# A mixture-of-experts loop: the next rows of a full block turned by VectorE in 16 pieces instead of by TensorE, and a slot table of one packed word

## The chip, the cores and the metric

One Trainium2 chip, one of its cores. The metric is the device time of one execution in microseconds; lower is better. The core's engines run side by side, each through its own queue in order: TensorE (PE, with its weight loads listed apart as PEld), VectorE (DVE), ScalarE (ACT), GpSimd (POOL) and SyncE (SP, which here mostly issues transfers).

## The reference

Eight batches of twelve heads, 448 tokens each, head width 64: sigmoid attention, whose output becomes 3584 rows of 768. A skip score and a gate then pick, for each row that is computed at all, one of eight experts; the others stay as they are.

```python
scores = scale * q @ k.T - log(S);  attn = sigmoid(scores);  x = attn @ v   # -> rows [3584, 768]
do = x @ w_skip > 0
e  = argmax(x[do] @ w_gate);  g = softmax weight of e
out = x;  out[do] = x[do] + g * (relu(x[do] @ w1[e]) @ w2[e])               # w1 [8,768,1024], w2 [8,1024,768]
```

How many rows each expert gets is known only on the chip, so the expert part is a loop whose blocks are chosen at run time.

## The kernel before

**Stages.** The attention fills the first half of the span and something more. While it runs, rows are written to `out`, and records (token number and gate weight) are sorted by expert into a list in DRAM. VectorE then computes a table of blocks ("slots"), while TensorE works through two first blocks of the largest early expert. After them comes the loop (L1549), one block an iteration, up to 128 rows of one expert in a block.

**Four kinds of block.** `FULL` and `SPLIT` (`block(i, last)`, L1347, with `last` False and True) compute 128 rows with weights split into a high and a low part, three matmuls in place of one, for precision: `gemm1` (L508) in 18 matmuls for each half of the hidden width, `gemm2` (L538) in six for each of eight slices `j`. `SPLIT` is the last full block before the expert changes: it also makes the high and low weights of the next expert, on ScalarE and VectorE. `HALF` (up to 64 rows, L1464) and `FEW` (up to 32, L1404) use unsplit weights of an expert of their own, which SP fetches for a later block while they run (`load_w1`, `load_w2`). The planner mixes them so that weights can arrive: in this run the loop goes SPLIT, HALF, FULL, HALF, FULL, FEW, FULL, FEW, FULL, FEW, SPLIT, FEW, FULL, FEW.

**What a FULL block does, in TensorE's order:** `gemm1(0)`; the first nine matmuls of `gemm1(1)`; `turn_h(0)` (four transposes of the hidden half 0); the other nine; `turn_x` of `xn`, the rows of the next block (six transposes of 128x128 into PSUM tiles `pxt`, L492); `gemm2(0)`; `turn_h(1)`; `gemm2(1)` to `gemm2(7)`. The order is written by hand (`tc.manual_schedule()`), so each engine's queue is in the order of the text.

**Around it.** ScalarE's `relu` and VectorE's share of `split_h` (L536) make `hh`/`hl`, the left operands of `gemm2`; each slice of `gemm2` uses `hl` in its last two matmuls. `ready_x` (L1120) reads the turned rows and makes `xh`, `xl`, `xf`, the next block's operands. `fetch` (L1279, on POOL) waits until `xn` has been read, then gathers the rows of the block after the next into `xn` and its records into `rn`; `take_rec` copies the records. At the end VectorE weighs the sums into `ys` (L1345, in a FEW block `yt`, L1460), `put` scatters them by an indirect transfer that adds (L570), and `advance` shifts the records. VectorE reaches a block only after it has finished this tail of the block before. In a FEW block the write of `yt` waits for the scatter of the block before.

**The table.** `slots` holds three numbers a slot: whether the block fetches an expert, which, and the kind. `entry` (L1103) loads one of them to a register. Every engine loads the kind at the head of an iteration; in HALF and FEW blocks SP loads the two others as well.

## Time and profile before

| | us |
|---|---|
| median of 3 runs (lowest, highest) | 528.02 (527.29, 532.5) |
| profiled execution, whole | 530.13 |
| its span, first to last instruction | 525.3 |
| TensorE busy in the span | 504.4 |
| VectorE busy | 293.4 |
| ScalarE busy | 272.3 |
| POOL busy | 259.0 |

The profile shows one execution. Its own time is 4.8 us above its span and 2.1 us above the median; differences are worked out within the span and then put on the median. In a timeline row the first number is the start in us, the second the time from the start of the first to the end of the last instruction of the row. The chain is followed back from the last instruction, at each step to what released it.

### The profile page before, as it was taken

The numbers are of one execution on the slowest core, as the hardware profiler recorded it, in microseconds if no ns is written. First come the engines' busy times: TensorE is split into PE (matmuls) and PEld (weight loads), VectorE is DVE, ScalarE is ACT, GpSimd is POOL, SyncE is SP. The second block draws the span as 40 slices with busy tenths as digits, with TensorE's granted clock in tenths as the row PEclk, the third lists the DMA queues.
The fourth block names the chain that finished last, engine by engine and source line by source line (L and its number), as shares of the span: only waits on it lengthen the run. The fifth ranks groups of instructions, "written<-read, shape, count | busy, mean of one in ns | idle before, by whom it ended". The sixth has DMA issues, their size and how long they took to land.

```text
span 525.3 us, 15167 instructions
## 1 busy us (share of the span) xinstructions
PE 504.4 (96%) x4982; PEld 332.6 (63%) x4983; DVE 293.4 (56%) x744; ACT 272.3 (52%) x480; POOL 259.0 (49%) x405
## 2 busy tenths in 40 slices
PE   8999999989999999999999999999999999999992
PEld 5555545545455555555555989948678787878771
DVE  4665647646668678488575862862122222249431
ACT  5776766757567666676675212942112323258311
POOL 5524463442555876667566332553224444446543
PEclk9999999999999999999999999999999999999997
DMA  7798576577688887878764133979393959595953
GB/s 235 180 266 216 157 180 156 147 161 194 170 223 219 211 204 221 196 193 251 193 125 100 17 93 122 375 226 334 97 372 117 347 199 350 203 351 203 327 190 47
DMA packets 139713, 107.23 MB, mean 204 GB/s; under 512 B 96263, under 2 KB 112265, under 8 KB 139664
## 3 DMA queue, kind: packets, MB, share of 16 engines
q1 hardware_dynamic: 133264, 97.66, 62.9%
q0 software_dynamic: 4736, 8.66, 7.3%
q8 instruction: 32, 0.52, 0.4%
q10 hardware_dynamic: 1664, 0.26, 0.3%
q14 instruction: 17, 0.14, 0.1%
HBM read 98.49 MB, written 17.60 MB: 221 GB/s over the span
## 4 chain that ended last, share of the span: by engine, by line
PE 92%; ACT 3%; DMA 2%; issue 1%; DVE 1%; POOLq 0%; POOL 0%; DVEq 0%; ACTq 0%
PE s L236 26%; PE pa L264 23%; PE py L543 11%; PE ph L516 10%; PE b_ph L516 3%; PE b_py L543 3%; PE py L1412 2%; DMA out_dram<-ys,rp 2%; PE ph L1412 2%; PE py L1470 2%; PE ph L1470 2%; PE pxt L492 2%; ACT at L256 2%; PE pl L296 2%; PE pht L530 1%
## 5 line engine op out<-in xcount | busy, mean ns | idle before, releaser
L256 ACT ACTIVATE at<-s,bias 128x896 f32<-128x896 f32 (+1 forms) x191 | 170.6, 914 | 85.0 <-PE s L236 79.1
L236 PE MATMUL s<-x 64*64 64x448 f32 (+1 forms) x1504 | 160.9, 497 | 5.8 <-ACT at L256 5.0
L264 PE MATMUL pa<-at,v 64*64 64x448 f32 (+1 forms) x1528 | 162.0, 489 | 0.0
L180 POOL COPY kq<-kq 32x896 f32<-32x896 f32 (+1 forms) x96 | 87.9, 915 | 80.3 <-DMA kq<-in_q_dram 41.8
L236 PEld LDWEIGHTS s<-x 64*64 64x64 f32 x1504 | 76.0, 191 | 62.2 <-ACT at L256 28.3
L264 PEld LDWEIGHTS pa<-at,v 64*64 64x64 f32 x1528 | 59.7, 133 | 57.8 <-issue 52.1
L216 DVE STREAM_TRANSPOSE x<-kq 128x448 f32<-128x448 f32 x94 | 82.1, 949 | 8.9 <-POOL kq L180 5.6
L274 DVE TENSOR_TENSOR xt<-xt,pa 128x448 f32<-128x448 f32 x48 | 29.8, 620 | 68.1 <-ACT xt L680 61.7
L486 POOL TENSOR_TENSOR wl<-wr,wh 128x384 fp32r<-128x384 f32 (+1 forms) x28 | 31.3, 1124 | 26.9 <-DVE wh L485 18.7
L413 POOL DMA_INDIRECT lst<-rec,idx x32 | 32.4, 1012 | 18.3 <-issue 13.5
L279 DVE STREAM_TRANSPOSE y<-xt 128x448 f32<-128x448 f32 x48 | 31.0, 646 | 1.6
L536 DVE TENSOR_TENSOR hl<-pht,hh 128x512 fp32r<-128x512 f32 x14 | 9.7, 690 | 37.6 <-ACT hh L535 32.7
L525 ACT ACTIVATE hs<-ph 128x512 f32<-128x512 f32 x14 | 8.4, 597 | 42.0 <-PE ph L516 34.1
L543 PE MATMUL py<-wh,hh 128*128 128x384 f32 x112 | 29.9, 348 | 0.0
L543 PE MATMUL py<-wh,hl 128*128 128x384 f32 x112 | 28.8, 338 | 0.2 <-DVE hl L536 0.2
L543 PE MATMUL py<-wl,hh 128*128 128x384 f32 x112 | 28.7, 337 | 0.0
L680 ACT ACTIVATE xt<-pa 128x448 f32<-128x448 f32 x48 | 25.7, 536 | 3.1 <-PE s L236 1.8
L516 PE MATMUL ph<-wl,xh 128*128 128x512 f32 x84 | 26.6, 403 | 0.0
L502 DVE TENSOR_TENSOR xl<-pxt,xh 128x384 fp32r<-128x384 f32 x30 | 15.3, 552 | 19.1 <-issue 9.6
L516 PE MATMUL ph<-wh,xh 128*128 128x512 f32 x84 | 25.7, 403 | 0.0
L1345 DVE TENSOR_SCALAR ys<-py,recs 128x384 f32<-128x384 f32 (+1 forms) x18 | 10.4, 612 | 26.0 <-PE py L543 20.7
L516 PE MATMUL ph<-wh,xl 128*128 128x512 f32 x84 | 24.4, 395 | 0.0
(291 smaller groups left out, 681.8 us busy)
## 6 DMA issues: line engine op xcount, KB each, us to landing
raw<-in_moe_w_dram SPq DMA_DIRECT2D x64, 768.0 KB
v<-in_v_dram SPq DMA_DIRECT2D x47, 256.0 KB
out_dram<-y SPq DMA_DIRECT2D x192, 56.0 KB
kq<-in_k_dram SPq DMA_DIRECT2D x23, 448.0 KB
kq<-in_q_dram SPq DMA_DIRECT2D x23, 448.0 KB
wr<-in_moe_w_dram SPq DMA_DIRECT2D x12, 256.0 KB
wr<-in_moe_w_dram SPq DMA_DIRECT2D x16, 192.0 KB
lst<-fill SPq DMA_DIRECT2D x4, 464.0 KB
```

The source lines that it names most:

```text
L180: nc.gpsimd.tensor_copy(a[to, :, :, :BT], a[at, :, :, BT:])
L216: nc.vector.transpose(xs[:, n].rearrange("p (r j) -> p j r", j=NJ), t.rearrange("p (j d) -> p j d", d=D)[:, :, :BT],)
L236: nc.tensor.matmul(sc[m * D : (m + 1) * D, j, : qs.stop - qs.start], xs[r, 0, first::NR7], xs[r, 1, qs], start=True, stop=True,)
L256: nc.scalar.activation(at[:, :, :n], sc[:, :, :n], AF.Sigmoid, bias=bias, scale=SCALE)
L264: nc.tensor.matmul(pa[j * D : (j + 1) * D, r, qs], vt[r][j][:, c if r == j else (c + 1) % NV, :], at[rs, j, : qs.stop - qs.start], start=( ...
L274: nc.vector.tensor_tensor(x, x, pa[:, 1, :S], op=ALU.add)
L279: nc.vector.transpose(y, xts[b][:, hp, :])
L413: put = nc.gpsimd.indirect_dma_start(out=lst[:, :], out_offset=bass.IndirectOffsetOnAxis(ap=idx[:, c : c + 1], axis=0), in_=rec[:, c, :], ...
L486: nc.gpsimd.tensor_tensor(lo, r, hi, op=ALU.subtract)
L516: nc.tensor.matmul(ph[h], a[:, j * P : (j + 1) * P], w[j][h], start=(n == 0), stop=(n == len(t) - 1),)
L543: last = nc.tensor.matmul(py[:, o, :H2], a[h][:, js], w[j][:, o * H2 : (o + 1) * H2], start=(j == 0 and n == 0), stop=(j == NK2 - 1 and n ...
L680: nc.scalar.activation(xts[b][:, hp, :], pa[:, 0, :S], AF.Copy)
```

## The change

In FULL blocks VectorE turns the next rows. `xn` (128 tokens by 768 columns) is taken in 16 pieces: 32 tokens by 192 columns, the columns being six runs of 32. One `transpose` turns its six 32x32 squares and writes them to one group of 32 partitions of a new tile `xw` in SBUF. Twelve pieces stand at the head of the block, ahead of everything VectorE does in it; four behind `take_rec`. `gemm2(0)` and `gemm2(1)` both stand ahead of `turn_h(1)`. `ready_x` reads `xw` there. The other three kinds turn as before. A slot is one word: 32 times the kind, plus 16 if an expert is fetched, plus the expert; SP takes the two fields out of the word that it loaded already.

```diff
+    W = 4 * NE
-    V.tensor_scalar(at5[:, 4], at5[:, 4], float(HALF - FEW), float(FEW), op0=ALU.mult, op1=ALU.add)
+    V.tensor_scalar(
+        at5[:, 4], at5[:, 4], float(W * (HALF - FEW)), float(W * FEW), op0=ALU.mult, op1=ALU.add
+    )
...
     V.tensor_reduce(at5[:, 2:4], w3d[:, 0:2], axis=AX.X, op=ALU.add)
+    V.scalar_tensor_tensor(
+        at5[:, 4], at5[:, 2], float(2 * NE), at5[:, 4], op0=ALU.mult, op1=ALU.add
+    )
+    V.tensor_tensor(at5[:, 4], at5[:, 4], at5[:, 3], op=ALU.add)
...
-    V.memset(f_hf, 0.0)
-    V.tensor_copy(kinds[:, :, :3], gt[:, :15].rearrange("p (n j) -> p n j", j=5)[:, :, 2:5])
+    V.tensor_copy(kinds[:, :, :1], gt[:, :15].rearrange("p (n j) -> p n j", j=5)[:, :, 4:5])
...
-    slots = const.tile([3, NS], I32, name="slots")
-    V.tensor_scalar(slots, ptab[:3, NS : 2 * NS], 0.25, None, op0=ALU.add)
+    slots = const.tile([1, NS], I32, name="slots")
+    V.tensor_scalar(slots, ptab[:1, NS : 2 * NS], 0.25, None, op0=ALU.add)
...
+    xw = mo.tile([P, NK1, P], F32, name="xw")
-    skip(4614 - 2 * H2)
+    skip(4614 - 2 * H2 - DM)
...
-    def next_expert(col):
-        return entry(NXT, col, SP, NE - 1), entry(HAS, col, SP, 1)
+    def next_expert(word):
+        return word & (NE - 1), (word & (2 * NE)) >> (2 * NE).bit_length() - 1
...
+    def turn_quads(x, ns):
+        rows = x.rearrange("t (i g j) -> t g i j", i=NK1, j=BT)
+        for b, g in [divmod(m, 4) for m in ns]:
+            nc.vector.transpose(
+                xw[g * BT : (g + 1) * BT, :, b * BT : (b + 1) * BT],
+                rows[b * BT : (b + 1) * BT, g],
+            )
...
+        if not last:
+            turn_quads(xn, range(12))
         gemm1(0, range(G1), xh, xl, ph, last)
         relu(0, hs, ph)
         split1(range(3), 0)
+        ahead = 1 if last else 2
         gemm1(1, range(9), xh, xl, ph, last)
         turn_h(0, hs, pht[0])
         split_h(0, pht[0], hh, hl)
         take_rec()
+        if not last:
+            turn_quads(xn, range(12, 16))
         split1(range(3, NK1), 0)
         gemm1(1, range(9, G1), xh, xl, ph, last)
         relu(1, hs, ph)
-        for h in range(2):
-            turn_x(xn, h, pxt[h])
+        if last:
+            for h in range(2):
+                turn_x(xn, h, pxt[h])
         fetch()
         split1(range(3), 1)
-        gemm2(0, hh, hl, py)
+        for j in range(ahead):
+            gemm2(j, hh, hl, py)
         turn_h(1, hs, pht[1])
...
-            ready_x()
-        for j in range(1, NK2):
+            ready_x([xw[:, 3 * h : 3 * h + 3].rearrange("p i t -> p (i t)") for h in range(2)])
+        for j in range(ahead, NK2):
             gemm2(j, hh, hl, py)
...
-        kind = entry(TYP, ds(i + 2, 1), mybir.ALL_ENGINES, SPLIT)
-        choose(kind, i)
+        word = nc.values_load(slots[0:1, ds(i + 2, 1)], min_val=0, max_val=W * (SPLIT + 1) - 1)
+        choose(word, i)
```

`choose` compares `word` with 32 times the kind where it compared the kind.

## The prediction

> **What bounds the kernel now.** First the page: span, engines, and the chain that ended last.

> ```profile
> span 525.3 us, 15167 instructions
> PE 92%; ACT 3%; DMA 2%; issue 1%; DVE 1%; POOLq 0%; POOL 0%; DVEq 0%; ACTq 0%
> ```

> TensorE carries 92% of the chain, so work taken from it shortens the time, as long as it isn't made to wait. Then the chain through a FULL block, and through the last one. Columns: start, us, what.

> ```profile
> 354.00 6.48 PE ph L516 x27
> ...
> 410.94 6.49 PE ph L516 x27
> ...
> 419.95 0.66 PE pxt L492 x6
> 420.60 1.05 PE py L543 x6
> ...
> 437.10 6.49 PE ph L516 x27
> ...
> 485.04 11.13 DMA out_dram<-ys,rp
> ...
> 496.26 0.13 DVE yt L1460
> ...
> 498.76 0.70 DVE hl L536
> ...
> 499.51 0.62 PE py L543 x2
> ```

> In most blocks the chain is TensorE back to back, and `turn_x` is 0.66 us of it. The last FULL block differs: its chain comes from a transfer, the scatter of the SPLIT block two blocks earlier, which takes 11.13 us. The FEW block's `yt` waits for it on VectorE, so VectorE reaches the FULL block so late that TensorE already waits for `hl` there. When it reaches each block, and when TensorE needs `hl`, the two timelines tell:

> ```profile
> 355.90 0.15 DVE L1338 CAST rid<-recs 128x1 int32<-128x1 f32 x1
> ...
> 413.90 0.15 DVE L1338 CAST rid<-recs 128x1 int32<-128x1 f32 x1
> 418.62 0.69 DVE L536 TENSOR_TENSOR hl<-pht,hh 128x512 fp32r<-128x512 f32 x1 [4.57 <-ACT hh L535]
> ...
> 497.30 0.15 DVE L1338 CAST rid<-recs 128x1 int32<-128x1 f32 x1
> ```

> ```profile
> 364.20 0.51 PE L543 MATMUL py<-wh,hl 128*128 128x384 f32 x2
> ...
> 421.14 0.51 PE L543 MATMUL py<-wh,hl 128*128 128x384 f32 x2
> ...
> 488.82 1.67 PE L516 MATMUL ph<-wh,xh 128*128 128x512 f32 x6
> ```

> The cast is the last instruction of the block before. The time from it to VectorE's first work in the next block is seen where that work is already waited for: 498.76 - 497.30 = 1.46 us, taken by the loop's end, the table load and the branches. So VectorE can begin at 357.36 in the block that starts at 354.0 (after HALF), at 415.36 in that of 410.9 (after FEW), and at 498.76 in that of 488.8, where the block is 9.9 us old. Of the five FULL blocks two follow HALF, three FEW; the one at 437.1 has the spacings of that at 410.9, the second after HALF those of the first.

> **What a piece costs.** The forms of VectorE's transposes, and two pairs of copies:

> ```profile
> L216 DVE STREAM_TRANSPOSE x<-kq 128x448 f32<-128x448 f32 x94 | 82.1, 949 | 8.9 <-POOL kq L180 5.6 <-remote 3.3
> L279 DVE STREAM_TRANSPOSE y<-xt 128x448 f32<-128x448 f32 x48 | 31.0, 646 | 1.6
> L309 DVE STREAM_TRANSPOSE lt<-pl 128x96 f32<-128x96 f32 x7 | 2.0, 283 | 8.7 <-PE pl L296 8.7
> ...
> L625 DVE STREAM_TRANSPOSE x_first<-kq_first 128x128 f32<-128x128 f32 x3 | 0.8, 376 | 0.0
> ...
> L625 DVE STREAM_TRANSPOSE x_first<-kq_first 128x64 f32<-128x64 f32 x1 | 0.3, 256 | 0.0
> ```

> ```profile
> 404.44 0.23 DVE L1335 COPY sv<-recs 128x2 f32<-128x2 f32 x2
> ...
> 407.00 0.32 DVE L1408 COPY gate<-recs 32x1 f32<-32x1 f32 x2 [1.90 <-issue]
> ```

> ```profile
> L1335 DVE COPY sv<-recs 128x2 f32<-128x2 f32 x24 | 2.7, 156 | 0.0
> ...
> L1408 DVE COPY gate<-recs 32x1 f32<-32x1 f32 x10 | 1.4, 142 | 7.7 <-issue 7.6
> ```

> Two forms with packed runs are 283 ns for 96 elements and 646 for 448: 1.03 ns an element, so 192 elements are 283 + 96 x 1.03 = 382 ns. How closely pieces follow each other, the copies bound from both sides. Two `sv` copies take 0.23 us together and 156 ns each, so the second starts 0.08 us before the first ends. Two `gate` copies take 0.32 together and 142 each: the second starts 0.036 us after the first ends. Neither pair depends on its own results; the `gate` pair writes to two different groups of 32 partitions. The pieces change the group they write at every step, so the `gate` row is the nearest: a piece takes 0.382 + 0.036 = 0.418 us, twelve 5.0 us. With overlap it would be 0.30 and twelve 3.6.

> [...]

> **The sum.** Removed: six transposes on TensorE, 0.65 us a block between its neighbours (419.95 to 420.60). In exchange `hl` is needed 0.65 earlier, and twelve pieces stand ahead of it. `hl` itself takes 0.69, and 0.06 pass until TensorE goes on (498.76 + 0.69 to 499.51).

> After HALF: 357.36 + 5.0 + 0.75 = 363.1, needed at 364.20 - 0.65 = 363.55. No wait; 0.65 gained, twice 1.3.

> After FEW, the blocks at 410.9 and 437.1: 415.36 + 5.0 + 0.75 = 421.1, needed at 420.5. A wait of 0.6 eats the gain: 0.03 each.

> The last: VectorE begins at 498.76 where `hl` began, so `hl` and all behind it in TensorE move by the whole twelve pieces: +5.0, and the 0.65 is worth nothing there, as TensorE waits anyhow.

> The table: two small dependent operations are added to VectorE's planning chain, behind the reduction that makes `at5[:, 2:4]`.

> ```profile
> 303.67 0.32 DVE L1023 TENSOR_REDUCE at<-arena 128x18 f32<-128x162 f32 x1
> 303.91 0.22 DVE L1026 SCALAR_TENSOR_TENSOR arena<-arena,slot 128x9 f32<-128x9 f32 x1
> ...
> 308.94 0.28 DVE L1085 SCALAR_TENSOR_TENSOR grids<-marks,arena,grids 128x64 f32<-128x64 bf16 x1
> ```

> ```profile
> 309.42 0.33 PE L1088 MATMUL ptab<-grids,ones_f 128*128 128x64 f32 x2
> ```

> The first must wait for the reduction's end, 303.99, where L1026 began at 303.91; with two such steps of some 0.2 L1026 comes 0.3 to 0.4 later. The chain ends at 309.22 and TensorE uses the result at 309.42, so nearly all of it is a wait: +0.3 (bounds 0 and 0.4). The removed memset overlaps other work.

> Sum: -1.3 - 0.06 + 5.0 + 0.3 = +3.9 us. The profiled execution becomes 534.0 (span 529.2), the median 528.02 + 3.9 = 531.9.

> **What is costed at nothing.** `fetch` now waits for the last four pieces (4 x 0.418 = 1.7 us) behind `hl`, so it starts up to 2.6 us later.

> ```profile
> 422.23 1.05 POOL L560 DMA_INDIRECT xn<-out_dram,rp  x1 [0.73 <-PE pht L530]
> ```

> ```profile
> 432.14 0.87 PE L492 MATMUL pxt<-ident,xn 128*128 128x128 f32 x6
> ```

> ```profile
> DMA packets 0, 0.00 MB, mean 0 GB/s; under 512 B 0, under 2 KB 0, under 8 KB 0
> ```

> The gather issued at 422.23 is used at 432.14, and the transfer view of 427.2 to 429 (third row) shows everything landed: 5 us of 9.9 used, so 2.6 is covered; beyond 4.9, TensorE would wait in the next block. The rows that the pieces themselves read were gathered in the HALF or FEW block:

> ```profile
> 409.14 1.07 POOL L560 DMA_INDIRECT xn<-out_dram,rp  x1 [0.74 <-PE py L1412]
> ```

> ```profile
> q1 hardware_dynamic: 557, 1.27, 105.6%
> ```

> In the transfer view of 415.4 to 418.6 only SP's queue moves, so this gather has landed by 415.4, when the pieces begin; each 0.1 later would cost 0.1. The four pieces behind `take_rec` end at 422.9, before the second `hl`: `gemm2(1)` moved ahead of `turn_h(1)` puts that at 423 or later, needed 2.1 us after `turn_h(1)`. `ready_x` from SBUF runs under `gemm2`, 5 us ahead of its use. SP's two table loads in HALF and FEW stand before waits for TensorE to leave the weights; their going moves no transfer.

> **The rivals.**

> Overlap: pieces at 0.30. No wait after FEW, four gains, the last block +3.6: -2.6 + 3.6 + 0.3 = +1.3, 529.3. For it: the `sv` pair, and that no piece waits for another. Against: the `gate` pair.

> Gaps (clearly slower): the pieces read and write in runs of 32 with gaps, and the forms with such patterns (L625) cost 376 - 256 = 120 ns for 64 elements, 1.9 each. 192 would be 376 + 120 = 496 ns, 0.53 with the gap, twelve 6.4. Then after FEW 415.36 + 6.4 + 0.75 - 420.5 = 2.0 of wait, net +1.4 twice, after HALF +0.3 twice, the last +6.4: with the table +10.1, 538.1. It decides against the kernel by over 1% from 0.454 us a piece on (three blocks then pay). Against it: those forms scatter single elements when writing, the pieces don't; L216 is 949 for 448.

> [...]

> On time (faster): the scatter of the SPLIT block lands as early as the others, and the last block is like the one at 410.9. Then -1.3 - 0.09 + 0.3 = -1.1, 526.9. For it: scatters depend on when weight transfers are issued. Against: nothing in SPLIT or FEW that sets that order is changed. With overlap too it would be -2.9, 525.1, all that the change can give.

> **How the numbers follow.** Forecast 0.56; overlap 0.17; gaps 0.12; on time 0.10 (with overlap 0.02 of it); anything else, such as a late gather, 0.05. The likeliest gives 531.9. The range holds overlap, on time and the forecast with pieces up to 0.47: 526.3 to 536.5; it leaves out gaps and the rest. A measurement of this kernel tells about 1%, 5.3 us, from no change: 0.454 us a piece reaches it. Slower by over 1%: gaps, the rest, and a fifth of the forecast (0.11): 0.28. Faster by over 1% isn't reached by any case: 0.03. Within: 0.69.

> **What would show it.** Sixteen transposes of 32x192 a block, mean near 382 ns, twelve in a row spanning 5.0 (3.6: overlap; 6.4: gaps). No L492 in FULL blocks; TensorE waiting for `hl` 0.6 us in the blocks after FEW, about 5 in the last, none after HALF. The scatter of the second SPLIT block still near 11 us on the chain. It would be wrong if that scatter lands early, or if the pieces wait for something that these rows don't show.

## The result

The changed kernel takes 532.78 us (median of 18 runs, 530.18 to 537.7), the kernel before on the same chip 528.08 (18 runs, 526.76 to 532.5): a ratio of 1.0079, 95% interval 1.0061 to 1.0097. Forecast were 531.9 us, +3.9; it became +4.7. (One run of the experiments, in e12, took 1321 us and is left out of its ratio.)

On other chips the numbers differ and are compared only within a chip: on three of them the kernel before takes 516 to 517 us. On one of these the changed kernel takes 533.09 against 516.55, a ratio of 1.032 (1.0293 to 1.0347). That is outside what was forecast, and the experiments are mostly about it.

### The profile page after: what moved, and what is told of

The parts are those of the page before. It is cut to its first block, busy times and chain, and to the rows that moved or that the text cites. A ratio compares the mean times of both kernels' runs of the same rounds, so it can differ in the third digit from the quotient of the medians.

```text
span 529.9 us, 15322 instructions
## 1 busy us (share of the span) xinstructions
PE 503.2 (95%) x4952; PEld 331.8 (63%) x4953; DVE 324.9 (61%) x825; ACT 273.6 (52%) x480; POOL 257.4 (49%) x405
## 4 chain that ended last, share of the span: by engine, by line
PE 85%; DVE 5%; DMA 3%; ACT 3%; issue 2%; DVEq 0%; POOLq 0%; POOL 0%; ACTq 0%
PE s L236 25%; PE pa L264 23%; PE py L543 11%; PE ph L516 7%; PE b_py L543 2%; PE b_ph L516 2%; DVE xw L1351 2%; PE ph L1428 2%; DMA out_dram<-ys,rp 2%; PE py L1428 2%; PE py L1486 2%; PE ph L1486 2%; PE pl L296 2%; ACT at L256 2%; PE pxt L492 1%
## 5 line engine op out<-in xcount | busy, mean ns | idle before, releaser
L180 POOL COPY kq<-kq 32x896 f32<-32x896 f32 (+1 forms) x96 | 87.9, 915 | 78.2 <-DMA kq<-in_q_dram 47.7
L216 DVE STREAM_TRANSPOSE x<-kq 128x448 f32<-128x448 f32 x94 | 82.1, 947 | 7.2 <-POOL kq L180 3.2
L413 POOL DMA_INDIRECT lst<-rec,idx x32 | 32.2, 1005 | 18.1 <-issue 13.3
L1351 DVE STREAM_TRANSPOSE xw<-xn 32x192 f32<-32x192 f32 x80 | 29.6, 370 | 10.9 <-issue 5.2
L543 PE MATMUL py<-wh,hl 128*128 128x384 f32 x112 | 29.8, 347 | 6.8 <-DVE hl L536 6.8
L279 DVE STREAM_TRANSPOSE y<-xt 128x448 f32<-128x448 f32 x48 | 31.0, 645 | 1.6
L543 PE MATMUL py<-wh,hh 128*128 128x384 f32 x112 | 29.8, 348 | 0.0
L543 PE MATMUL py<-wl,hh 128*128 128x384 f32 x112 | 29.1, 341 | 0.0
L516 PE MATMUL ph<-wl,xh 128*128 128x512 f32 x84 | 26.6, 403 | 0.0
L1283 POOL TENSOR_TENSOR xn<-xn,zf 128x1 f32<-128x1 f32 x14 | 4.5, 323 | 44.5 <-PE py L543 24.9
L516 PE MATMUL ph<-wh,xh 128*128 128x512 f32 x84 | 25.7, 403 | 0.0
L543 PEld LDWEIGHTS py<-wh,hl 128*128 128x128 f32 x112 | 20.6, 193 | 7.9 <-DVE hl L536 7.8
L1346 DVE TENSOR_SCALAR ys<-py,recs 128x384 f32<-128x384 f32 (+1 forms) x18 | 10.4, 612 | 23.1 <-PE py L543 17.8
```

The costliest lines, as they stand in the source:

```text
L180: nc.gpsimd.tensor_copy(a[to, :, :, :BT], a[at, :, :, BT:])
L216: nc.vector.transpose(xs[:, n].rearrange("p (r j) -> p j r", j=NJ), t.rearrange("p (j d) -> p j d", d=D)[:, :, :BT],)
L279: nc.vector.transpose(y, xts[b][:, hp, :])
L413: put = nc.gpsimd.indirect_dma_start(out=lst[:, :], out_offset=bass.IndirectOffsetOnAxis(ap=idx[:, c : c + 1], axis=0), in_=rec[:, c, :], ...
L516: nc.tensor.matmul(ph[h], a[:, j * P : (j + 1) * P], w[j][h], start=(n == 0), stop=(n == len(t) - 1),)
L543: last = nc.tensor.matmul(py[:, o, :H2], a[h][:, js], w[j][:, o * H2 : (o + 1) * H2], start=(j == 0 and n == 0), stop=(j == NK2 - 1 and n ...
```

## The profile after

Lines of the changed kernel have moved: pieces L1351, `yt` L1476, `ys` L1346, `take_rec` L1343. From its page, span and the engines of the chain that ended last; from its list of instructions, the group of the pieces (count, busy us and mean ns, idle time before).

```profile
span 529.9 us, 15322 instructions
...
PE 85%; DVE 5%; DMA 3%; ACT 3%; issue 2%; DVEq 0%; POOLq 0%; POOL 0%; ACTq 0%
...
L1351 DVE STREAM_TRANSPOSE xw<-xn 32x192 f32<-32x192 f32 x80 | 29.6, 370 | 10.9 <-issue 5.2 <-DMA xn<-out_dram,rp 3.4
```

TensorE's share of the chain falls from 92% to 85%, VectorE's rises from 1% to 5%: some of the path now leads through the pieces. The span grew by 4.6 us. The profiled execution as a whole grew by 1.45 only, to 531.58: it lies 1.7 us above its span, where that of before lay 4.8 above. Next VectorE's timeline, a row each for a block after HALF, one after FEW and the last, with the `hl` behind the pieces:

```profile
357.37 4.77 DVE L1351 STREAM_TRANSPOSE xw<-xn 32x192 f32<-32x192 f32 x12 [1.85 <-issue]
362.17 0.69 DVE L536 TENSOR_TENSOR hl<-pht,hh 128x512 fp32r<-128x512 f32 x1
...
440.24 4.78 DVE L1351 STREAM_TRANSPOSE xw<-xn 32x192 f32<-32x192 f32 x12 [1.86 <-DMA xn<-out_dram,rp]
445.05 0.69 DVE L536 TENSOR_TENSOR hl<-pht,hh 128x512 fp32r<-128x512 f32 x1
...
497.41 4.77 DVE L1351 STREAM_TRANSPOSE xw<-xn 32x192 f32<-32x192 f32 x12 [1.51 <-issue]
502.21 0.69 DVE L536 TENSOR_TENSOR hl<-pht,hh 128x512 fp32r<-128x512 f32 x1
```

Twelve pieces take 4.77 or 4.78 us in all five FULL blocks. These blocks start at 353.39, 435.30 and 487.42, so `hl` begins 8.8, 9.75 and 14.8 us into them. What follows on TensorE in the last one, and its clock (windows: length, busy us and instructions of PE, PEld, DVE, ACT, POOL, then the granted clock, DMA share and GB/s):

```profile
502.95 1.01 PE L543 MATMUL py<-wh,hl 128*128 128x384 f32 x2 [5.73 <-DVE hl L536]
503.76 0.84 PE L543 MATMUL py<-wh,hh 128*128 128x384 f32 x2
```

```profile
501.00:502.00 1.00, 0.00 (x0) 0.00 (x0) 0.93 (x3) 0.00 (x0) 0.00 (x0) 1.00 1.09 306
502.00:503.00 1.00, 0.05 (x1) 0.05 (x1) 0.94 (x3) 0.00 (x0) 0.00 (x0) 0.70 0.96 384
503.00:504.00 1.00, 1.00 (x3) 1.00 (x4) 0.93 (x3) 0.00 (x0) 0.36 (x3) 0.50 0.33 132
504.00:505.00 1.00, 1.00 (x4) 1.00 (x4) 0.55 (x2) 0.00 (x0) 0.76 (x6) 0.50 0.24 95
505.00:506.00 1.00, 1.00 (x6) 0.90 (x6) 0.00 (x0) 0.00 (x0) 0.40 (x1) 0.60 0.01 3
506.00:507.00 1.00, 1.00 (x9) 1.00 (x7) 0.00 (x0) 0.48 (x1) 0.69 (x2) 1.00 0.00 0
```

TensorE waits 5.73 us for `hl`, and then runs at half clock (0.50) for almost 3 us. The chain there (start, us, what) begins as before, with the SPLIT block's scatter, and now has the pieces behind it:

```profile
483.73 10.89 DMA out_dram<-ys,rp
...
494.71 0.13 DVE yt L1476
...
497.41 0.37 DVE xw L1351
...
502.21 0.70 DVE hl L536
```

## The experiments

First their outcome together: how long each FULL block lasted, from its first matmul to that of the next block, read off TensorE's timelines. (In e5 the blocks behind them are longer as well.)

| kernel | before's median on its chip | two after HALF | two after FEW | last |
|---|---|---|---|---|
| before, first chip | 528.1 | 18.53, 18.53 | 18.54, 18.56 | 19.07 |
| after, first chip | 528.1 | 17.90, 17.92 | 18.58, 18.87 | 25.18 |
| e1 table only | 516.6 | 18.53, 18.55 | 18.56, 18.56 | 18.83 |
| e2 early scatter | 516.6 | 17.92, 17.90 | 22.87, 23.12 | 25.07 |
| e3 eight and eight | 516.6 | 17.90, 17.90 | 21.67, 20.56 | 23.62 |
| e4 same output group | 516.6 | 17.90, 17.90 | 23.24, 23.83 | 25.16 |
| e5 behind | 516.6 | 21.34, 21.22 | 23.27, 21.20 | 23.08 |
| e6 few rows | 516.6 | 17.90, 17.90 | 19.38, 19.48 | 24.04 |
| e7 after again | 516.6 | 17.90, 17.90 | 24.74, 24.01 | 25.29 |
| e8 before again | 516.6 | 18.56, 18.56 | 18.53, 18.56 | 18.54 |
| e9 sum on POOL, eight | 530.0 | 17.88, 17.90 | 18.25, 18.48 | 23.91 |
| e10 sum on POOL | 530.0 | 17.91, 17.89 | 19.80, 19.75 | 25.77 |
| e11 no w1 in FEW | 530.0 | 17.90, 17.90 | 19.30, 19.31 | 24.98 |
| e12 table again | 516.2 | 18.55, 18.56 | 18.52, 18.54 | 18.67 |

e1 to e4 shared a chip, e5 to e8 another, e9 to e11 a third; e12 had a fourth.

### e1 and e12: the table alone

```diff
-        if not last:
-            turn_quads(xn, range(12))
...
-        if last:
-            for h in range(2):
-                turn_x(xn, h, pxt[h])
+        for h in range(2):
+            turn_x(xn, h, pxt[h])
```

> The changed kernel with the turn put back: FULL blocks turn the next rows on TensorE where they did before, in the old order; only the packed table is left. Theory (all of the loss comes from the twelve pieces in the last FULL block): the table costs some 0.3 us on TensorE's wait for the slot table ahead of the loop and nothing in the loop: 528.4, ratio 1.0005, all five FULL blocks 18.5 to 19.1 us as before. Rival (the table or its longer planning chain is a good part of the 4 us): 530 or more, with a wait of over 1 us at the table's matmul or longer HALF and FEW blocks.

`gemm2(0)` alone stands ahead of `turn_h(1)`, and `ready_x` reads `pxt`, as before. Measured: 514.29 us against 516.59, ratio 0.9955 (0.9939 to 0.9972). The FULL blocks are as expected; the whole is not +0.3 us but a small gain.

> The packed slot table alone again, TensorE turning the rows as before, on whatever chip these runs get. Theory (the table takes 2 to 3 us off the time that lies outside the span and costs the span nothing): profiled time less span 1.6 to 2.0 us, where the kernel before had 3.7 and 4.8; full blocks 18.5 us throughout and 19 in the last; 0.993 to 0.998 of before. Rival (0.9955 came from a late weight load in one few block of before on that chip): 0.999 to 1.002 here.

Measured: 514.82 against 516.2, ratio 0.9971 (0.9956 to 0.9986). So a gain of 1.4 to 2.3 us is there on two chips, and on such chips this version beats both kernels. The gain lies outside the span. In the median of the runs on each chip the time outside it went from 3.87 to 1.75 us with e1 and from 3.75 to 1.71 with e12; the span itself went from 512.7 to 512.4 and from 512.4 to 513.0, so the forecast +0.3 within it is neither shown nor refuted. In the profiles, kernels with the packed table took 1.7 to 2.0 us outside in eleven of twelve executions (3.6 in e11), the kernel before 4.8 and 3.7. What is saved there the traces don't show.

### e2: the scatter of SPLIT earlier

```diff
         put(P)
+        if last:
+            for h in range(2):
+                lo_x(h, pxt[h], xh, xl)
         advance(1 if last else 2)
         if last:
-            for j in range(4, NK2):
+            for j in range(3, NK2):
                 lo2(j)
```

`lo_x` and one `lo2` of SPLIT move behind its `put`.

> The changed kernel with one thing moved in SPLIT blocks: VectorE weighs the sums, and the scatter goes out, ahead of the next block's low rows and of the low parts of w2 from the fourth on, instead of behind them; the scatter is issued about 1 us earlier. Theory (VectorE comes late to the last FULL block because that scatter, issued behind the first weight loads, lands late): if the scatter now gets through before the weights, VectorE reaches the last FULL block some 4 to 5 us earlier, the wait for hl there falls from 6 us to 1 or less, and the time to 527 to 528, ratio 0.998 to 1.000. If it still lands 8 us into the block, the time stays at 532 to 533, and the issue order of 1 us isn't what makes it late. Rival (the pieces cost by themselves, wherever VectorE begins): 531 or more even with the scatter early.

Measured: 529.78, ratio 1.0260 (1.0232 to 1.0288): the expectation failed twice over. The SPLIT block's scatter went out 4.1 us ahead of the last FULL block (from 486.28) instead of 2.6 (e4, same chip), and `yt` begins 5.2 us into that block instead of 6.9. It still waits 2.44 us for the scatter, which lands at 491.37 (the row names ScalarE's `hs`, which `yt` doesn't read). But then the pieces wait for the gather of their own rows. VectorE's timeline:

```profile
491.46 0.61 DVE L1477 SCALAR_TENSOR_TENSOR yt<-py,gate,yh 64x384 f32<-64x384 f32 x1 [2.44 <-ACT hs L525]
495.47 4.76 DVE L1351 STREAM_TRANSPOSE xw<-xn 32x192 f32<-32x192 f32 x12 [2.82 <-DMA xn<-out_dram,rp]
```

And the two FULL blocks after FEW, which the edit doesn't touch, take 4.3 and 4.6 us more than e1's. Two things were thus missing from the theory: a late gather, and late scatters in FEW blocks that follow FULL.

### e3: eight pieces ahead, eight behind

```diff
-            turn_quads(xn, range(12))
+            turn_quads(xn, range(8))
...
-            turn_quads(xn, range(12, 16))
+            turn_quads(xn, range(8, 16))
```

> The changed kernel with 8 pieces at the head of a FULL block and 8 behind the first hl, in place of 12 and 4. Theory (each piece ahead of the first hl costs 0.40 us in the last block, and the two blocks after FEW wait for their last pieces): the last block gains 4 x 0.40 = 1.6 us and perhaps the 1.3 us of half clock, the two blocks after FEW 0.6 and 0.9: 2.6 to 4.4 less than the changed kernel, 528.5 to 530, ratio 1.001 to 1.004. Rival (the number of pieces matters, not their place): unchanged, 532 to 533.

Measured: 525.21, ratio 1.0166 (1.0149 to 1.0183). The expected 1.001 to 1.004 is missed, since on this chip three blocks are late and not one. Four pieces fewer ahead of `hl` are worth 1.5 to 3.3 us in each block that is late (against e4). After HALF, where VectorE is on time, eight or twelve make no difference (17.90 us).

### e4: pieces in a row with one output group

```diff
-        for b, g in [divmod(m, 4) for m in ns]:
+        for g, b in [divmod(m, 4) for m in ns]:
```

> The changed kernel with the order of the pieces turned round: four pieces in a row write to the same 32 partitions and read from four different ones (before: read from the same, write to four). [...] Rival A (only a change of the output group holds a piece): nine of twelve overlap, 0.29 apart, 12 in 3.8 us. [...]

Measured: 530.42. Twelve pieces on VectorE's timeline:

```profile
407.17 4.76 DVE L1351 STREAM_TRANSPOSE xw<-xn 32x192 f32<-32x192 f32 x12 [1.51 <-ACT hh L535]
```

4.76 us for twelve of 0.370 is again 0.400 from start to start, though nine of the eleven steps now stay in one output group. Rival A is out. What sets the 0.030 us between two pieces these runs don't show.

### e7 and e8: both kernels on a faster chip

Neither is edited.

> The changed kernel unaltered, for its blocks on the chip of these runs. If the late scatter after full blocks belongs to the chip of the first experiments, that chip gives about 1.025 of before, with the three full blocks behind a few block at 23 to 25 us; on a chip like that of the first profile 1.008, with only the last of them late.

> The kernel before unaltered, for its blocks on the chip of these runs. Theory: its yt waits for the scatter in the same few blocks as the changed kernel's, but the full blocks behind them stay at 18.5 to 19.1 us, since nothing stands ahead of hl. Rival (the change itself moved the scatter later): in it yt waits only in the last of them.

Measured: e7 533.09, ratio 1.032 (1.0293 to 1.0347), three FULL blocks late; e8 516.96. In e7, SP's two groups of weight loads, POOL's scatter and gather, and VectorE in the FEW block that starts at 393.17 and the FULL block behind it (400.16):

```profile
394.91 3.86 SPq L1231 DMA_DIRECT2D raw<-in_moe_w_dram  x4
399.66 4.75 SPq L1240 DMA_DIRECT2D raw<-in_moe_w_dram  x4
```

```profile
395.34 1.63 POOL L570 DMA_INDIRECT out_dram<-ys,rp  x1 [0.58 <-issue]
...
399.10 1.07 POOL L560 DMA_INDIRECT xn<-out_dram,rp  x1 [0.74 <-PE py L1428]
```

```profile
405.53 0.61 DVE L1476 SCALAR_TENSOR_TENSOR yt<-py,gate,yh 64x384 f32<-64x384 f32 x1 [5.35 <-DMA out_dram<-ys,rp]
...
408.22 4.77 DVE L1351 STREAM_TRANSPOSE xw<-xn 32x192 f32<-32x192 f32 x12 [1.50 <-ACT hh L535]
413.02 0.69 DVE L536 TENSOR_TENSOR hl<-pht,hh 128x512 fp32r<-128x512 f32 x1
```

The scatter is issued by 397.0 and `yt` gets it 8.5 us later, behind SP's loads. Now the same place in e12, where TensorE turns the rows:

```profile
406.27 0.61 DVE L1471 SCALAR_TENSOR_TENSOR yt<-py,gate,yh 64x384 f32<-64x384 f32 x1 [5.14 <-DMA out_dram<-ys,rp]
...
408.89 0.69 DVE L536 TENSOR_TENSOR hl<-pht,hh 128x512 fp32r<-128x512 f32 x1 [1.43 <-ACT hh L535]
```

The same wait, 5.14 us, and the FULL block (from 401.16) still takes 18.52: with nothing ahead of `hl` it begins 7.7 us into the block. A late VectorE was harmless; the pieces ahead of `hl` make it count. So the pieces are not what makes the scatters late. The packed table may well be. In e8, the kernel before, `yt` waits so long after the first FEW block only (5.22 us), after the next three 0.5 to 1.1; so e8's expectation failed there, while its FULL blocks held (18.53 to 18.56). In e1 and e12, which have the table and not the pieces, `yt` waits 3.3 to 5.7 us after all four. The second FEW block shows what differs: scatter, first loads and `yt` in e8 (block from 418.92), then in e12 (from 419.68):

```profile
421.08 1.62 POOL L570 DMA_INDIRECT out_dram<-ys,rp  x1 [0.58 <-issue]
422.82 3.14 SPq L1230 DMA_DIRECT2D raw<-in_moe_w_dram  x4
426.64 0.61 DVE L1460 SCALAR_TENSOR_TENSOR yt<-py,gate,yh 64x384 f32<-64x384 f32 x1 [0.73 <-ACT yh L1459]
```

```profile
421.84 1.62 POOL L570 DMA_INDIRECT out_dram<-ys,rp  x1 [0.58 <-issue]
422.34 3.73 SPq L1231 DMA_DIRECT2D raw<-in_moe_w_dram  x4
430.06 0.61 DVE L1471 SCALAR_TENSOR_TENSOR yt<-py,gate,yh 64x384 f32<-64x384 f32 x1 [3.37 <-DMA out_dram<-ys,rp]
```

SP comes late to this block in both. In e8 three table loads stand ahead of its weight loads, which go out 3.9 us into the block, 1.7 behind the start of the scatter. In e12 one table load does, and they go out after 2.7 us, 0.5 behind it. In e7 they go out 1.74 us into each of these blocks, ahead of the scatter. So the rival of e8's expectation, that the change moved the scatter later, stands; with one trace of the kernel before on these chips it isn't shown. On the first chip both kernels issue these loads 1.74 us into the three FEW blocks behind FULL, ahead of the scatter, and yet `yt` begins 2.0 us into the next block. Why the scatter lands sooner there is not settled; SP's second group of loads is issued 6.5 us into the FEW block in e7, on the first chip 8.8:

```profile
403.17 4.48 SPq L1231 DMA_DIRECT2D raw<-in_moe_w_dram  x4
410.27 3.91 SPq L1240 DMA_DIRECT2D raw<-in_moe_w_dram  x4
```

(the changed kernel on the first chip, FEW block from 401.43).

### e6: a scatter of eight rows

```diff
-            out_rows = scatter(rp[0][:n], ys[:n], ALU.add)
+            m = 8 if n == P else n
+            out_rows = scatter(rp[0][:m], ys[:m], ALU.add)
```

> The change as it is, but the full and split blocks scatter 8 of their 128 rows (120 rows of the output are left unwritten). Theory: yt no longer waits for that scatter, so VectorE reaches every full block on time, and with 12 pieces still ahead of hl the last full block takes 17.9 to 18.6 us instead of 25.2, the total 6 to 8 us under that of the changed kernel on the same chip. Rival (the 12 pieces themselves make hl late there, the wait is a companion): the last full block stays over 23 us.

Measured: 519.26 where e7 takes 533.09 on the same chip. The blocks after FEW fall to 19.4, not to 17.9, the last to 24.0 only. From e6's timelines of VectorE and TensorE (block from 398.77):

```profile
401.44 0.61 DVE L1477 SCALAR_TENSOR_TENSOR yt<-py,gate,yh 64x384 f32<-64x384 f32 x1 [2.66 <-DMA out_dram<-ys,rp]
...
404.23 4.77 DVE L1352 STREAM_TRANSPOSE xw<-xn 32x192 f32<-32x192 f32 x12 [1.60 <-DMA xn<-out_dram,rp]
```

```profile
409.77 0.62 PE L543 MATMUL py<-wh,hl 128*128 128x384 f32 x2 [1.21 <-DVE hl L536]
```

Fewer bytes help, but even eight rows land 6 us after they are issued, where 128 rows took 8.5: size is only part of it. And the gather is the next to be waited for. In the last block the rival's sign came (over 23 us), but by way of that gather: the pieces wait for it until 8.6 us into the block.

### e5: no piece ahead of hl

```diff
-        if not last:
-            turn_quads(xn, range(12))
...
-            turn_quads(xn, range(12, 16))
+            turn_quads(xn, range(8))
...
         split_h(1, pht[1], hh, hl)
+        if not last:
+            turn_quads(xn, range(8, 16))
```

The second eight stand behind `fetch`, so they turn rows 64 to 127 of what the same block fetches; only blocks of up to 64 rows follow here.

> The change with none of the 16 pieces ahead of hl: 8 behind the first hl and 8 behind the second. Theory (pieces cost only where VectorE reaches a full block late and they stand ahead of hl): hl is on time in every full block, wherever the scatter lands; each full block about 18.0 us instead of 18.53, the last 18.0 to 18.6 instead of 25.2; no half clock in the last full block; 0.988 to 0.996 of before. Rival 1 (the pieces cost VectorE or its port, wherever they stand): the last full block stays over 22 us and the whole at 1.00 or above. Rival 2 (the second eight push xh and xf past the block's end): every full block 18.5 to 20, 1.000 to 1.010.

Measured: 538.81, ratio 1.043 (1.0406 to 1.0455). The first `hl` was on time as expected, 7.8 us into four blocks and 9.5 into the last. But the edit made a new wait, so the times of the blocks say nothing on the theory: the second eight wait for the new gather, ScalarE for them, TensorE's next block for ScalarE. Timelines of VectorE, ScalarE and TensorE:

```profile
363.33 3.18 DVE L1351 STREAM_TRANSPOSE xw<-xn 32x192 f32<-32x192 f32 x8 [3.58 <-DMA xn<-out_dram,rp]
```

```profile
366.63 0.94 ACT L498 ACTIVATE xh<-xw 128x384 fp32r<-128x384 f32 x2 [7.60 <-DVE xw L1351]
```

```profile
367.96 1.22 PE L1486 MATMUL ph<-raw,xf 128*64 128x512 f32 x2 [3.37 <-ACT xf L1114]
```

With `hl` free of pieces the blocks are long for another reason. A version that turns the right rows behind `hl` has to hold `fetch` back; that wasn't tried.

### e9 and e10: the wait for the scatter moved to POOL

```diff
-        nc.vector.scalar_tensor_tensor(yt, py[:MD, 0, :H2], gate2, yh, op0=ALU.mult, op1=ALU.add)
+        nc.scalar.activation(yu, py[:MD, 0, :H2], AF.Copy, scale=gate2)
+        pool.tensor_tensor(yt, yu, yh, op=ALU.add)
```

> The change with two edits: FEW's last sum moves from VectorE to POOL (ScalarE scales the lower half as well, POOL adds the halves into yt), so that the wait for the full block's scatter stands on POOL and not on VectorE; and 8 pieces stand ahead of hl and 8 behind it. Theory (two things make the pieces late behind a few block: yt's wait on VectorE, and the gather of xn, which shares the scatter's queue and lands about 5.7 us into the block): eight pieces from 5.8 us on end by 9.1, when hl is due, so every full block takes 17.9 to 18.5, the last at most 20; 0.988 to 0.998 of before. Rival (the scatter harms by something else than VectorE's place, and moving the sum only moves the wait): full blocks behind few blocks stay at 20 to 24 as with eight and eight alone, 1.012 to 1.02.

> The same move of FEW's last sum to POOL, with the change's own 12 and 4 pieces. If yt's wait alone makes VectorE late: full blocks behind few blocks 17.9 to 18.1, total about 511 where the kernel before takes 516.5. If the gather of xn is late as well, as the theory has it: the first piece about 5.7 to 6 us into the block, twelve of 0.4 us end 1.5 us after hl is due, these blocks 19.3 to 20.5, total 514 to 519. If neither: 23 to 25 us as in the changed kernel, total 530.

Measured: e9 534.49 against 529.99, ratio 1.0066 (1.0039 to 1.0094); e10 540.44. The chip was one like the first, where the blocks after FEW were nearly on time already. e9's stay under 18.5. e10's, at 19.8, lie in the range given for a late gather, but for another reason: there, too, VectorE waits for POOL (3.9 us, until 417.62 in the first of them). The last, at 24 to 26, fails both expectations. In e9's last FULL block, from 490.72, on POOL and VectorE:

```profile
497.76 1.00 POOL L1478 TENSOR_TENSOR yt<-yu,yh 64x384 f32<-64x384 f32 x1 [2.72 <-DMA out_dram<-ys,rp]
```

```profile
499.26 0.15 DVE L1340 CAST rid<-recs 128x1 int32<-128x1 f32 x1 [6.53 <-POOL rs L1308]
500.92 3.16 DVE L1352 STREAM_TRANSPOSE xw<-xn 32x192 f32<-32x192 f32 x8 [1.50 <-ACT hs L525]
```

In the last block the wait only changed its name: `advance` may not overwrite `rid` until POOL has read it, and POOL now stands behind the scatter.

### e11: no loads of w1 in FEW

```diff
-        for h in range(2):
-            for g in range(2):
-                load_w1(g, h, nx)
```

> The changed kernel with the four loads of w1 left out of FEW (its later full blocks use stale weights). Theory: the scatter and the gather behind it are late because their packets come behind these loads; without them both land within 4 us of their issue, yt waits under 1 us, and the full blocks behind few blocks take 17.9 to 18.1; total 509 to 514 where before takes 516.5. Rival (the scatter's own packets or its queue are slow): these blocks stay at 23 to 25 us and the scatter still lands about 10 us after its issue.

Measured: 551.06, but its loop began 7 us later than e9's and its first SPLIT block took 22.1 us, so only the blocks are read. The last FULL block (from 504.86), VectorE:

```profile
507.37 0.61 DVE L1473 SCALAR_TENSOR_TENSOR yt<-py,gate,yh 64x384 f32<-64x384 f32 x1 [1.10 <-DMA out_dram<-ys,rp]
...
513.65 4.77 DVE L1351 STREAM_TRANSPOSE xw<-xn 32x192 f32<-32x192 f32 x12 [4.00 <-DMA xn<-out_dram,rp]
```

Half of the theory holds: without the w1 loads `yt` waits 1.1 us for the scatter, where it waited 5.9 in the changed kernel on the first chip. The gather, issued two microseconds after SP's w2 loads, is now what is late, and the block still takes 24.98, not 18.

## Why the prediction was right, and where it wasn't

**A piece, and the spacing.** 382 ns and 0.418 us were forecast, 370 and 0.400 measured; twelve 5.0 and 4.77. Overlap (3.6) and gaps (6.4) are both out, and the view that decides is the one named: twelve in one row. The reason that was given for the spacing, a new output group at every step, isn't borne out: with two such steps in eleven it is 0.400 as well (e4).

**After HALF.** -0.65 each; measured -0.63 and -0.61, with no wait for `hl`. In every kernel with 8 or 12 pieces ahead it is 17.9. One term was too small: from the cast to the first piece VectorE took 2.01 us (355.36 to 357.37) and not 1.46. The shorter pieces made up for 0.2 us of it, and `hl` came just in time where the forecast had 0.45 us to spare.

**After FEW.** -0.03 each; measured +0.04 and +0.31; TensorE's waits for `hl` there are 0.41 and 0.69, where 0.6 was forecast. The 0.27 more in the second is a step that failed in small: the gather had not "landed when the pieces begin"; the row at 440.24 above waits for it. The forecast had read the gather in one of the two blocks and taken the other for the same; in the trace of before it lands there at 441.95, 0.4 us after VectorE could have begun (440.08 + 1.46).

**The last FULL block.** +5.0; measured +6.11, with the scatter still on the chain at 10.89 us. The step itself held: `hl` begins 4.85 us later in the block than before (9.94, now 14.79). What was mis-sized is what follows from it: TensorE, idle for 5.73 us, comes back at half clock, some 1.3 us more (the block takes what `hl` has plus 10.39, where it is 9.12 at full clock).

**The reason for it was only half the reason.** The forecast had VectorE late because `yt` waits for the scatter. But e2, e9 and e11 each shorten that wait or move it, and the block stays at 24 to 25: the gather of the pieces' own rows lands 8 to 9 us into that block too. TensorE used to turn these rows late enough not to notice. Either is enough.

**Why it pays by the microsecond** is seen across the runs. Where `hl` begins up to 8.8 us into a block, the block takes 17.90. Later, it takes what `hl` has plus 9.12:

| kernel, block | hl begins at | block takes | difference |
|---|---|---|---|
| after, after FEW | 9.47 | 18.58 | 9.11 |
| after, after FEW | 9.75 | 18.87 | 9.12 |
| e9, after FEW | 9.36 | 18.48 | 9.12 |
| e6, after FEW | 10.26 | 19.38 | 9.12 |
| e10, after FEW | 10.69 | 19.80 | 9.11 |
| e3, after FEW | 11.45 | 20.56 | 9.11 |
| e3, after FEW | 10.98 | 21.67 | 10.69 |
| e2, after FEW | 12.29 | 22.87 | 10.58 |
| after, last | 14.79 | 25.18 | 10.39 |
| e7, after FEW | 12.86 | 24.74 | 11.88 |

The last four include stretches at half clock.

**The table.** +0.3 forecast, a gain of 1.4 to 2.3 us measured (e1, e12), outside the span, which the sum hadn't looked at. On the first chip the loop grew by 5.15 us (the FULL blocks' +5.22), the stretch ahead of it shrank by 0.55. "Their going moves no transfer" held on the first chip; on the others the weight loads went out earlier, as e12 beside e8 shows.

**The total is near in part by luck.** The sum of +3.9 was made for the span and put on the median as it stood. If the packed table saved some 2 us outside the span on the first chip too, as it did in e1 and e12, then the span grew by nearer 6.7 us in the median (4.7 + 2.0, an estimate; in the profiled pair it grew by 4.6). A gain that the sum didn't have stands against losses that it had too small.

**The rivals.** The range goes further than its reason: at 0.47 us a piece the sum makes 534.3, not 536.5. "On time" had the scatter late in one block or none. The other direction wasn't considered: on a faster chip (e7) the scatters of the FULL blocks are late as well, three blocks pay, and the whole is +3.2%. The forecast held on the chip from which its rows came.

## What to carry to other kernels

Before moving work to the head of an engine's queue, look at how late that engine, and the work's own input, arrive there in every block, not only where they wait today: slack that an engine used up silently becomes time on the path when something is put ahead of its first urgent result. Taking away one late arrival is worth nothing if a second ends at the same time; here scatter and gather, both issued by POOL near SP's weight loads, were late for the same block (e11, with no w1 loads: `yt` waits 1.1 us for the scatter, and then the pieces 4.0 for the gather). An engine that gets to its transfers sooner may put them ahead of others that were in time (SP's loads go out 1.7 us behind the scatter's start in e8 and 0.5 in e12; `yt` waits 3.4 us for the scatter in e12, and only 0.7, for ScalarE, in e8). And a wait that is hidden on one chip can be seen on another (a ratio of 1.0079 on the first chip, 1.032 on e7's), so a forecast from one trace holds for the kind of chip that made it.

## What the runs showed of the hardware

```profile
412.00:413.00 1.00, 0.29 (x2) 0.29 (x3) 0.97 (x3) 0.00 (x0) 0.12 (x1) 1.00 1.02 402
413.00:414.00 1.00, 1.00 (x7) 1.00 (x7) 0.91 (x4) 0.00 (x0) 0.54 (x4) 0.89 1.03 406
414.00:415.00 1.00, 1.00 (x6) 0.90 (x5) 0.35 (x1) 0.00 (x0) 0.00 (x0) 0.50 0.83 329
...
417.00:418.00 1.00, 1.00 (x7) 1.00 (x7) 1.00 (x4) 1.00 (x7) 0.97 (x2) 0.90 0.72 172
```

A mean of 0.89 and of 0.90 in the outer windows put the stretch from 413.78 to 417.20: 3.4 us. In the changed kernel it is 3.4 as well (502.4 to 505.8, from its 0.70 and 0.60), in e7's last block 6.8 (501.75 to 508.6), twice that.

The length of the gap does not decide alone: in e3 one of 1.93 us had a half-speed stretch behind it and one of 2.41 had none. Where the gap lies may count. In the changed kernel's trace the clock falls at 502.39 and again, behind the last matmul of the loop, at 522.87: 20.48 us later, six times 3.41. In e3 the half-speed stretch begins at 412.13 (a mean of 0.57 from 412 to 413). Counted from there in steps of 3.41, the gap of 1.93 lies in one step (the first row), and the next runs at half clock; the gap of 2.41 falls on two, with 0.78 and 1.63 us idle (the last two rows):

```profile
408.72:412.13 3.41, 1.48 (x8) 1.07 (x7) 3.16 (x10) 0.60 (x1) 0.00 (x0) 1.00 1.04 390
...
436.03:439.44 3.41, 2.63 (x13) 1.95 (x11) 2.16 (x6) 1.07 (x2) 1.36 (x1) 1.00 1.04 400
439.44:442.85 3.41, 1.78 (x11) 1.75 (x12) 3.16 (x10) 0.00 (x0) 0.00 (x0) 1.00 1.04 387
```

In the changed kernel the 3.41 us ahead of the fall at 502.39 are idle throughout; the 3.41 before them have 1.76 us idle, with no fall behind. That the place of the gap decides is a reading of these few cases; no run moved a gap to test it.

**Indirect transfers came late where weight loads were issued near them**: `yt` saw a scatter of eight rows 6 us after its issue (e6) and one of 128 rows 8.5 us after (e7); with no w1 loads near it, one of 128 rows was seen after 4 (e11: issued by 503.4, `yt` at 507.37), and with the loads 1.7 us behind the scatter's start `yt` found it landed 3.9 us after its issue (e8: by 422.70, `yt` at 426.64). On the first chip, with the loads 0.4 us ahead of it, one of 128 rows had landed within 5.8 (after: issued by 405.22, `yt` at 411.02, released by ScalarE).
